# First projections in blocks of 128 rows with a packed rest, lead-in loads shared with SyncE, gradient row copies in the first stage

## The chip, the core and the metric

The kernel runs as one program on one core of a Trainium2 chip. The metric is device time in microseconds (us) of that core; of several runs the median counts. TensorE is called PE in the profile (PEld is its weight load), VectorE DVE, ScalarE ACT, GpSimd POOL and SyncE SP. DMAs are issued from three engines, each with a queue of its own: SP (q1), ACT (q10) and POOL (q0).

## The reference

The kernel computes a forward pass and all gradients of a block with two branches that share a normalized input. Cut to what matters:

```python
xn = layernorm(x)                                  # 2048 tokens x 640
# branch A: 64 segments of 32 tokens; 8 memory rows are carried from one to the next
for s in range(64):
    h = concat([mem, xn[32*s:32*s+32]])            # 40 rows
    q, k, v = h @ Wq, h @ Wk, h @ Wv               # 32 heads x 128
    o = softmax(mask(q @ k.T * 128**-0.5)) @ v
    o = o @ Wo
    mem, out_s = o[:8], o[8:]
# branch B: gated MLP, inner width 1728
g = silu((silu(xn @ w1) * (xn @ w3)) @ w2)
out = x + concat(out_s) * g
# returned: out, and by vjp(grad_out) the gradients of x, mem0, Wq, Wk, Wv, Wo, w1, w3, w2
```

## The kernel before

The program is a row of stages. Inside each of the stages below a helper `in_order` fixes the written order for every engine, so an engine never starts an instruction before the one written ahead of it, and a DMA that has to wait holds up what is written behind it on the same issuing engine. Only semaphores tie the engines together.

**Forward of branch B and the first projections of V** (`phase12_ln_Bfwd`, 0 to 284 us). Layernorm, then the MLP in four blocks of 512 tokens. On the way the normalized rows are copied from DRAM to DRAM into `HRO` in one strided DMA (`x_rows`, L252) on SP. Behind the last block `first_rows` (L358 to L372) computes V for the first 672 tokens (`NB0`) in six blocks of 112 rows. For each block and each of four column groups (`cg`) there are two PSUM banks of 512 columns, and each bank takes five matmuls (L367), one for each 128 of the 640 input features. VectorE evicts the one bank and ScalarE the other into a staging tile `b0st`, and a DMA (L372) stores it. The remaining tokens get their projections one segment at a time in the recurrence, where they ride along with the memory rows.

**First projections of K and Q** (`first_part`, 284 to 407 us). The same `first_rows`, twice 24 steps, counted by `n`. The stores go out on POOL from four staging tiles. In the same steps SP stores the transposed V weights to the DRAM tensor `WVT` (`turn_w`; the tiles lie in a ring of six slots), ACT issues the fetches of Wq and Wo (`fetch`, every other step), POOL clears tiles and loads the memory rows (`mem_ld`), and PE turns the first K rows (`kload`, `kturn`).

**Recurrence** (407 to 1703 us) and a stage of output projections follow. In the recurrence the function `packed_half` (L302 to L308) multiplies 32 rows with four column groups at once: four matmuls of 32 columns of the array each write one quarter of a bank's partitions.

**Backward recurrence** (`phase4_Abwd`, 1888 to 3088 us). It begins with a lead-in of 19 units (`pro`) without a chain. A unit is four heads of up to three segments. Its `ld` loads `qv` (two pieces, L1194 for the memory rows and L266 for the token rows), `gor` (L266) and `Pr` (L1198). In the lead-in `gor` is loaded from SP, and the others from POOL (`early`). `turn` transposes V and the gradient rows; ScalarE copies V out of PSUM (L1209, L1210, two buffers), and POOL stores it to `VTD` (L1211). `dsoft` ends with a store to `DSR` (L1242) on POOL, `gmem` with a store to `GXP` (L1258) on SP. A step `i` of the lead-in does `turn(i)`, `dprob(i-1)`, `dsoft(i-1)`, `gmem(i-2)`, then loads unit `i+4`; in the first eight steps SP also loads an eighth of `WvT` from `WVT`, 640 KB each, and half of a block of `gx_block` (L843) is computed. After the lead-in the chain runs from segment 63 to 0. Behind each step below segment 54 POOL issues one DMA of the list `later` (L1349). Its first two entries copy the gradient rows `GS` to `GWO` from DRAM to DRAM: 21 tiles of 96 rows, 2.58 MB, and a rest of 32 rows. In the chain a step's staging tile `gstg` is stored to `GOS` from SP (L1100), and the same buffer is used again by `fup` (L335) late in the step.

**Weight gradients of branch A** (`phase6_Awgrads`, from 3088 us). Units in the order of `order`; `ld` brings five pieces per unit, and `s1` is the first PE work of a unit (L1426, transposes of `dS`). SP issues the loads of units 0 to 2, then `ld_w(0)`: three weight tiles of 4 heads, the first a plain load from `WVT` (L1394), the other two DMA transposes of Wk and Wq (L271), then the loads of units 3 and 4.

Of the kernel before, what the change touches and what calls it, by code (L numbers as in the profile page):

```python
# [16 lines left out]
P = 128  # L17
# [23 lines left out]
class K:  # L41
# [109 lines left out]
    def setup_dram(self):  # L151
        tc = self.tc
        S, D, T, H, F = self.S, self.D, self.T, self.H, self.F
        HD = self.HD
        dp = self.ctx.enter_context(tc.tile_pool(name="scratch", bufs=1, space=bass.MemoryType.DRAM))
        self.dp = dp
        mk = lambda name, shape, dt=BF16: dp.tile(list(shape), dt, name=name, uniquify=False)
        self.XN = mk("XN", (S, D))
        self.SLT = mk("SLT", (F, S))
        self.DUT = mk("DUT", (F, S))  # L160
        self.HB = mk("HB", (F, S))
        self.DZ = mk("DZ", (S, D))
# [24 lines left out]
        self.GL = 2 * P  # L187
        self.GX0 = mk("GX0", (S - self.GB0, HD))
        self.OR = mk("OR", (self.NTL * 120, HD))
        self.PR, self.DSR, self.VTD = [], [], []  # L190
        self.GXP = mk("GXP", (self.NTL, P, 8, 3, 2, 32), F32)
        for tl in range(self.NTL):
            n = self.geo(tl)[3]
            self.PR.append(mk(f"PR{tl}", (n, H, P)))
            self.DSR.append(mk(f"DSR{tl}", (n, H, P)))
            ns, nm = self.geo(tl)[0:2]
            self.VTD.append(mk(f"VTD{tl}", (P, ns, H, 40)))
        self.PM = mk("PM", (T, P, 80))
        self.GSP = mk("GSP", (8, 3, 160, 512))
        self.WVT = mk("WVT", (P, H, D))  # L200

    def x_src(self, tl, w, c0, c1):
        return self.tok_src(96 * tl, self.geo(tl)[2], w, c0, c1)
# [46 lines left out]
    def x_rows(self, A, X, eng):  # L250
# [2 lines left out]
                      X[0:96 * n, :].rearrange("(t r) d -> t r d", r=96))  # L253
        eng.dma_start(A[120 * n:120 * n + 32, :], X[96 * n:self.S, :])


    def g_src(self, tl, c0, c1):
        nx = self.geo(tl)[2]
# [10 lines left out]
def turned_load(k, dst, src):  # L269

    k.nc.sync.dma_start_transpose(dst, src)  # L271
# [83 lines left out]
    return pt  # L355


def first_rows(k, ps, stage, xs, off, W, dst, x0, cg, nb=112, tag="b0pb", w=1024, q=None):  # L358

    nc = k.nc  # L360
    for b in range(2):
        c0 = cg * 1024 + b * 512
        if w == 512 or b == 0:
            st = stage()
        pb = ps.tile([nb, 512], F32, name="b0pb", tag=tag)
        for dc in range(k.DC):
            nc.tensor.matmul(pb[:], xs[:, dc, x0 - off:x0 - off + nb], W[:, dc, c0:c0 + 512],  # L367
                             start=(dc == 0), stop=(dc == k.DC - 1))
        s0 = b * 512 if w == 1024 else 0
        k.copy(st[:, s0:s0 + 512], pb[:], eng='vs'[b])  # L370
        if w == 512 or b == 1:
            (q or nc.sync).dma_start(dst[x0:x0 + nb, cg * 1024 + (b * 512 if w == 512 else 0):cg * 1024 + b * 512 + 512], st[:])  # L372


def phase3_Afwd(k, W4, Wv, Wk_):
# [18 lines left out]
def first_part(k, Wv, Wk_, Wq, Wo, kTs, vt, hxs, rest):  # L394
    nc, tc = k.nc, k.tc
    DC, H, HD = k.DC, k.H, k.HD
    with tc.tile_pool(name="b0", bufs=1) as io, tc.tile_pool(name="b0s", bufs=4) as stp, \
# [14 lines left out]
        def mem_ld():  # L412
            nc.gpsimd.dma_start(k.m_rows(k.HRO, 0), k.mem0)
            with nc.allow_non_contiguous_dma(reason="tiny mem0 transpose load"):
                for dc in range(DC):
                    nc.gpsimd.dma_start(hxs[0][:, dc, 0:8], k.mem0[:, dc * P:(dc + 1) * P].rearrange("m p -> p m"))
# [31 lines left out]
            turn_w()  # L448
        n = 0
        for W, dst in ((Wk_, k.KX[:, :]), (Wq, k.QVX[:, 0])):  # L450
            for x0 in range(0, k.NB0, 112):
                for cg in range(4):
                    if n % 2 == 1 and fetch:
                        nc.scalar.dma_start(*fetch.pop(0))
                    first_rows(k, ps, lambda: stp.tile([112, 1024], BF16, name="b0st", tag="b0st"), xs, 0, W, dst, x0, cg, q=nc.gpsimd)
                    turn_w()
                    if zero:
                        nc.gpsimd.memset(zero.pop(0)[:], 0.0)
                    if n >= 26 and n % 2 == 0 and (n - 26) // 2 < 9:
                        i = (n - 26) // 2  # L460
                        if i > 0:
                            kturn(i - 1)
                        if i < 8:
                            kload(i)
                    if n == 20:
                        mem_ld()
                    if n == 30:
                        assert not turns
                        nc.gpsimd.memset(kTs[1][:], 0.0)
                    if n == 44:  # L470
                        for i in range(2):
                            nc.sync.dma_start(vt[64 * i + 8:64 * i + 40, :], k.QVX[0:32, 1, 2048 * i:2048 * i + 2048])
                    n += 1
# [375 lines left out]
def phase3b_out(k, Wo, W0, W4):  # L849
# [12 lines left out]
    with tc.tile_pool(name="oio", bufs=1) as io, tc.tile_pool(name="oac", bufs=1, space=bass.MemoryType.PSUM) as pa, \  # L862
# [96 lines left out]
        while g0:  # L959
# [2 lines left out]
        in_order(k, start)  # L962
    WT["v"] = W4.tile([P, H, D], BF16, name="WvT", tag="w3")

    n = k.NTL - 1
    later = [(k.GWO[0:120 * n, :].rearrange("(t r) d -> t r d", r=120)[:, 0:96], k.GS[0:96 * n, :].rearrange("(t r) d -> t r d", r=96)),
             (k.GWO[120 * n:120 * n + 32, :], k.GS[96 * n:k.S, :])]

    for s in range(3):
        t0 = (2, 0, 1)[s]  # L970
# [14 lines left out]
def phase4_Abwd(k, out2, WoT, WvT, WkT, WqT, later):  # L985
# [3 lines left out]
    with tc.tile_pool(name="gst", bufs=1) as st, tc.tile_pool(name="gchain", bufs=1) as ch, \  # L989
# [185 lines left out]
        def ld(tl, qd, eng=None):  # L1175

            ns, nm, nx, n = k.geo(tl)
            c0, h0 = qd * 512, qd * 4
            i = cnt["l"]
            cnt["l"] += 1  # L1180
            early = i < len(pro)
            g = i % 6 if early else (i - len(pro) + 1) % NG
            if g < NG:
                gor = gors[g][:]
                qv = fl.tile([120, 2, 512], BF16, name="gqv", tag="gqv", bufs=4)[:]
                Pr = fl.tile([120, 4, P], BF16, name="gPr", tag="gPr", bufs=4)[:]
            else:
                x = xb[:, g - NG]
                qv = x[:, 0:1024].rearrange("p (i c) -> p i c", i=2)
                gor = x[:, 1024:1536]  # L1190
                Pr = x[:, 1536:2048].rearrange("p (h c) -> p h c", h=4)
            t0 = 3 * tl
            q = nc.gpsimd if early else nc.sync
            q.dma_start(  # L1194
                qv[nx:n], k.QVM[t0:t0 + ns, :, qd // 2, :, 512 * (qd % 2):512 * (qd % 2) + 512].rearrange("t r i c -> (t r) i c"))
            k.load_x(qv, 0, k.x_src(tl, "qv", c0, c0 + 512), q)
            k.load_x(gor, 0, k.g_src(tl, c0, c0 + 512), nc.sync)
            q.dma_start(Pr[0:n], k.PR[tl][:, h0:h0 + 4, :])  # L1198
            uu["l", tl, qd] = qv, gor, Pr

        def turn(tl, qd):
# [152 lines left out]
def phase6_Awgrads(k, X, out0, out3, out4, out5):  # L1354
# [12 lines left out]
    with tc.tile_pool(name="h6i", bufs=3) as io, tc.tile_pool(name="h6", bufs=1) as hp, \  # L1367
# [20 lines left out]
        def ld_w(qd):  # L1388
            c0 = qd * 512
            ws = []  # L1390
            for i, src in enumerate((k.A_Wv, k.A_Wk, k.A_Wq)):
                w = gp.tile([P, 4, D], BF16, name="w6", tag=f"w6{i}")
                if i == 0:
                    nc.sync.dma_start(w[:], k.WVT[:, 4 * qd:4 * qd + 4, :])  # L1394
                else:
                    turned_load(k, w[:], src.rearrange("d h e -> d (h e)")[:, c0:c0 + 512])
                ws.append(w)
            Ws[qd] = ws
# [261 lines left out]
def phase12_ln_Bfwd(k: K, Wv, Wk_):  # L1660
# [6 lines left out]
    with tc.tile_pool(name="bw", bufs=1) as wp, tc.tile_pool(name="bio", bufs=2) as io, \  # L1667
# [162 lines left out]
                            up_ld(blk - 1, fc // 2 + 1)  # L1830
        hidden_out(NBLK - 1)
        xb = io.tile([P, DC, BLK], BF16, name="xnT_b", tag="xnT_b")
        turned_load(k, xb[:, :, 0:224], k.XN[448:672, :])
        up_ld(NBLK - 1, 0)
        up_ld(NBLK - 1, 1)
        xa, off = xnTs[NBLK], 0
        stg = []

        def stage():
            stg.append(ln.tile([112, 512], BF16, name="b0st", tag=f"xt{len(stg) % 8}"))  # L1840
            return stg[-1]
        for n, (x0, cg) in enumerate([(x0, cg) for x0 in range(0, k.NB0, 112) for cg in range(4)]):
            if n % 3 == 1 and n // 3 < TB:
                up(NBLK - 1, n // 3)
                if n < 6:
                    up_ld(NBLK - 1, n // 3 + 2)
            if x0 == 448:
                xa, off = xb, 448
            first_rows(k, ps, stage, xa, off, Wv, k.QVX[:, 1], x0, cg, tag="pg", w=512)
        in_order(k, start)  # L1850


# [271 lines left out]
```

## Time and profile before

| | |
|---|---|
| median of 4 runs | 4889.42 us (4886.75 to 4896.51) |
| the profiled execution | 4891.41 us, its span 4889.7 us |
| busy over the span | PE 93%, PEld 59%, DVE 45%, POOL 41%, ACT 34% |
| DMA | 841 MB, 172 GB/s |

Busy time by stage, from the profile's windows:

| stretch, us | what | PE busy, us | PE clock | DMA share | GB/s |
|---|---|---|---|---|---|
| 205 to 290 | end of branch B, V projections | 75.4 of 85 | 0.99 | 0.49 | 144 |
| 290 to 407 | K and Q projections | 115.3 of 117 | 0.98 | 0.71 | 241 |
| 1893 to 1972 | lead-in of the backward recurrence | 59.2 of 79 | 0.63 | 0.81 | 228 |
| 1975 to 3075 | backward recurrence | 1039.0 of 1100 | 0.98 | 0.71 | 200 |
| 3075 to 4300 | weight gradients of A and what follows | 1190.4 of 1225 | 0.98 | 0.52 | 137 |

A time is that of one whole execution; the span goes from the first to the last instruction of the profiled one. Busy means that at least one instruction of the engine was under way. The clock is the share of full speed that TensorE was granted. The DMA share is the mean busy share of the core's 16 DMA engines; it is modelled and can pass 1.

### The profile page before, as it was taken

What the parts mean: (1) busy time and instruction counts of PE and PEld (TensorE: products, weight loads), DVE (VectorE), ACT (ScalarE), POOL (GpSimd) and SP (SyncE); (2) the same over time, 40 slices, a digit from 0 to 9 for tenths busy, and PEclk for the clock granted to TensorE, in tenths of its full rate; (3) what the DMA queues carried; (4) which work ended last, traced back from release to release, by engine and by line L of the source; (5) the groups of instructions that cost most, each with busy time, mean ns of one, the idle gap of its engine ahead of it and who ended that gap; (6) DMA issues with size and microseconds to landing.
All of it is one profiled execution on the core that took longest, in us unless ns stands there. A gap on an engine that the chain in (4) does not pass through costs nothing. (4 is left out here: it accounts for less than half of the span.)

```text
span 4889.7 us, 160881 instructions
## 1 busy us (share of the span) xinstructions
PE 4543.8 (93%) x64704; PEld 2889.5 (59%) x64704; DVE 2221.5 (45%) x7189; ACT 1686.9 (34%) x4784; POOL 2003.7 (41%) x3384
## 2 busy tenths in 40 slices
PE   8899999999999867889999999799999999999999
PEld 4455555555555554556666665566666666667675
DVE  8634555555555523445555554332333323311461
ACT  5432555555555432323333332222333222300000
POOL 6522444444444313445544444533455334411440
PEclk9999999999999977999999999899999999999999
DMA  8663555555555478677777775743554434659784
GB/s 268 228 231 110 162 169 165 169 163 165 168 160 163 136 166 211 198 202 215 218 211 208 208 204 165 167 121 109 149 152 134 119 107 135 185 173 225 163 182 96
DMA packets 1010341, 841.32 MB, mean 172 GB/s; under 512 B 555979, under 2 KB 893375, under 8 KB 1007591
## 3 DMA queue, kind: packets, MB, share of 16 engines
q1 hardware_dynamic: 783175, 552.52, 41.4%
q0 software_dynamic: 129328, 227.22, 15.9%
q10 hardware_dynamic: 97091, 51.28, 4.2%
q8 instruction: 511, 8.37, 0.8%
q14 instruction: 236, 1.93, 0.1%
HBM read 473.80 MB, written 311.48 MB: 161 GB/s over the span
## 5 line engine op out<-in xcount | busy, mean ns | idle before, releaser
L1505 PE MATMUL wg<-gr,hr 128*128 128x512 bf16 x2400 | 521.7, 379 | 0.0
L1486 PE MATMUL g<-w,ghacc 128*128 128x320 bf16 x3072 | 460.4, 300 | 0.8
L1505 PEld LDWEIGHTS <-hr 128*128 128x128 bf16 x2400 | 233.9, 98 | 278.8
L1486 PEld LDWEIGHTS <-ghacc 128*128 128x128 bf16 x3072 | 288.8, 98 | 104.5 <-ACT ghacc L92 2.2
L738 POOL DMA_DIRECT2D OR<-xv x163 | 93.1, 571 | 446.8 <-ACT xv L737 340.8
L307 PEld LDWEIGHTS <-hx 128*32 128x32 bf16 x7680 | 178.2, 96 | 164.5 <-issue 4.6
L90 DVE CAST wgo<-wg 128x512 bf16<-128x512 f32 x72 | 49.8, 692 | 471.2 <-PE wg L1505 463.2
L90 DVE CAST stg<-bank 128x512 bf16<-128x512 f32 x256 | 177.1, 692 | 183.3 <-PE bank L307 177.7
L92 ACT COPY ghacc<-t6g 128x768 bf16<-128x768 bf16 (+1 forms) x176 | 137.1, 779 | 310.3 <-PE t6g L1468 309.3
L689 ACT ACTIVATE xP<-xsp,xnm 120x120 bf16<-120x120 f32 (+1 forms) x704 | 239.9, 374 | 9.0 <-DVE xnm L685 5.7
L326 PEld LDWEIGHTS <-gkv 128*8 128x8 bf16 x8192 | 178.1, 87 | 84.5 <-issue 4.4
L1211 POOL DMA_DIRECT2D VTD<-gvT x176 | 129.3, 742 | 226.9 <-ACT gvT L1210 205.1
L1451 POOL DMA_DIRECT2D GSP<-grs x48 | 25.7, 548 | 478.3 <-ACT grs L1443 477.5
L700 POOL TENSOR_TENSOR xP<-xP,xrz 120x480 bf16<-120x480 bf16 x163 | 161.8, 993 | 123.3 <-ACT xP L689 82.9
L92 ACT CAST wgo<-wg 128x512 bf16<-128x512 f32 x48 | 28.1, 585 | 479.8 <-PE wg L1505 392.5
L1492 DVE TENSOR_TENSOR ghacc<-ghacc,g 128x320 f32<-128x320 f32 x192 | 93.5, 487 | 209.7 <-PE g L1486 209.7
L1240 DVE SCALAR_TENSOR_TENSOR gdS<-gdp,Dx,gPr 120x120 bf16<-120x120 f32 (+1 forms) x680 | 183.0, 331 | 0.0
L564 DVE COPY vt<-stg 8x512 bf16<-8x512 bf16 x512 | 163.6, 320 | 21.0 <-ACT stg L92 13.5
L1258 POOL DMA_DIRECT2D GXP<-gks x157 | 91.6, 583 | 195.6 <-ACT gks L1256 186.9
L326 PE MATMUL bank<-Wo,oTm 128*32 128x320 bf16 x4032 | 170.4, 321 | 0.4
L326 PE MATMUL gbank<-WvT,gkv 128*8 128x320 bf16 x4096 | 169.5, 309 | 0.6 <-DVE gkv L1082 0.6
L326 PE MATMUL gbank<-WkT,gkv 128*8 128x320 bf16 x4096 | 162.0, 299 | 5.2 <-issue 3.4
(348 smaller groups left out, 10968.5 us busy)
## 6 DMA issues: line engine op xcount, KB each, us to landing
QVS<-stg SPq DMA_DIRECT2D x128, 256.0 KB
vTt<-VTD SPq DMA_DIRECT2D x64, 320.0 KB
VTD<-gvT POOLq DMA_DIRECT2D x168, 120.0 KB, 4.1
DSR<-gdS POOLq DMA_DIRECT2D x168, 120.0 KB, 3.4
dS<-DSR SPq DMA_DIRECT2D x168, 120.0 KB
P<-PR SPq DMA_DIRECT2D x168, 120.0 KB
PR<-xP POOLq DMA_DIRECT2D x163, 120.0 KB, 3.3
OR<-xv POOLq DMA_DIRECT2D x163, 120.0 KB, 2.5
```

Source lines behind the costliest of these rows:

```text
L90: return nc.vector.tensor_copy(out, in_)
L92: return nc.scalar.copy(out, in_)
L307: k.nc.tensor.matmul(bank[32 * g:32 * g + 32, :], x[:, dc, :], W[:, dc, c0:c0 + 512], start=(dc == 0), stop=(dc == k.DC - 1), tile_positio ...
L326: k.nc.tensor.matmul(pm[p0:p0 + nq, 0:320], x[:, h, :], W[:, h, 320 * b:320 * b + 320], start=(first and i == 0), stop=(last and i == 15), ...
L564: nc.vector.tensor_copy(vt[p0:p0 + 8, c0:c0 + 512], sv[32 * g:32 * g + 8, b * 512:(b + 1) * 512])
L689: nc.scalar.activation(Pb[0:n, j, 0:n], sp[0:n, j, :], ACT.Exp, bias=nmx[0:n, j:j + 1], scale=k.scale, accum_out=Z[0:n, j:j + 1])
L700: eng.tensor_tensor(Pb[0:n, :, 0:n], Pb[0:n, :, 0:n], bc_last(rz[0:n], n), ALU.mult)
L1211: nc.gpsimd.dma_start(k.VTD[tl][:, :, h0:h0 + 4, :], vTq[:])
L1240: nc.vector.scalar_tensor_tensor(dS[0:n, j, 0:n], dp[0:n, j, :], Dx[0:n, j:j + 1], Pr[0:n, j, 0:n], op0=ALU.subtract, op1=ALU.mult)
L1486: nc.tensor.matmul(pg[:], ring[:, i, j, r0:r0 + P], Ws[qd][i][:, j, 320 * h:320 * h + 320], start=(i == 0 and j == 0), stop=(i == 2 and j ...
L1492: nc.vector.tensor_tensor(a, a, pg[:], ALU.add)
L1505: nc.tensor.matmul(pw[:], hr[:, tl, dc * P:(dc + 1) * P], grs[i][:, tl, :], start=(tl == 0), stop=(tl == NF - 1))
```

## The change

- `first_rows` takes blocks of 128 rows: five blocks (640 rows). The last 32 rows go through a new function `last_rows`, which uses `packed_half`. The counters at which loads are issued in `first_part` move with the shorter loop (42 steps in place of 48).
- The copies of `GS` to `GWO` leave the list `later`. They are issued from SP in `first_part` at steps 10, 12, 14 and 16, as copies of 6, 6, 6 and 3 tiles and the rest (`x_part`).
- In their places in `later` stand two stores of 640 KB each from the resident transposed Wk and Wq to a new DRAM tensor `WQK`; `ld_w(0)` loads them in place of the two DMA transposes.
- In the lead-in's loads, the token rows of `qv` and `Pr` are issued from SP; the memory rows of `qv` stay on POOL.

```diff
+        self.WQK = mk("WQK", (2, P, 4, D))
...
+    def x_part(self, A, X, i, eng):
+        n = self.NTL - 1
+        h = (n + 3) // 4
+        t0, t1 = h * i, min(h * i + h, n)
+        eng.dma_start(A[120 * t0:120 * t1, :].rearrange("(t r) d -> t r d", r=120)[:, 0:96],
+                      X[96 * t0:96 * t1, :].rearrange("(t r) d -> t r d", r=96))
+        if i == 3:
+            eng.dma_start(A[120 * n:120 * n + 32, :], X[96 * n:self.S, :])
...
-def first_rows(k, ps, stage, xs, off, W, dst, x0, cg, nb=112, tag="b0pb", w=1024, q=None):
+def first_rows(k, ps, stage, xs, off, W, dst, x0, cg, tag="b0pb", w=1024, q=None):
...
-        pb = ps.tile([nb, 512], F32, name="b0pb", tag=tag)
+        pb = ps.tile([P, 512], F32, name="b0pb", tag=tag)
         for dc in range(k.DC):
-            nc.tensor.matmul(pb[:], xs[:, dc, x0 - off:x0 - off + nb], W[:, dc, c0:c0 + 512],
+            nc.tensor.matmul(pb[:], xs[:, dc, x0 - off:x0 - off + P], W[:, dc, c0:c0 + 512],
...
+def last_rows(k, ps, stage, xs, off, W, dst, tag="b0pb", w=1024, q=None):
+    x0 = k.NB0 - 32
+    for b in range(2):
+        if w == 512 or b == 0:
+            st = stage()
+        pb = ps.tile([P, 512], F32, name="b0pb", tag=tag)
+        packed_half(k, pb, xs[:, :, x0 - off:x0 - off + 32], W, b)
+        s0 = b * 512 if w == 1024 else 0
+        k.copy(st[:, s0:s0 + 512], pb[:], eng='vs'[b])
+        if w == 512 or b == 1:
+            c0, c1 = (b * 512 if w == 512 else 0), b * 512 + 512
+            (q or k.nc.sync).dma_start(dst[x0:k.NB0].rearrange("r (g c) -> g r c", g=4)[:, :, c0:c1], st[:])
...
-            for x0 in range(0, k.NB0, 112):
-                for cg in range(4):
+            for x0 in list(range(0, k.NB0 - 32, P)) + [None]:
+                for cg in range(4 if x0 is not None else 1):
...
-                    if n >= 26 and n % 2 == 0 and (n - 26) // 2 < 9:
-                        i = (n - 26) // 2
+                    if n >= 22 and n % 2 == 0 and (n - 22) // 2 < 9:
+                        i = (n - 22) // 2
...
-                    if n == 20:
+                    if n == 18:
                         mem_ld()
+                    if 10 <= n < 18 and n % 2 == 0:
+                        k.x_part(k.GWO, k.GS, (n - 10) // 2, nc.sync)
...
-                    if n == 44:
+                    if n == 38:
...
-    n = k.NTL - 1
-    later = [(k.GWO[0:120 * n, :].rearrange("(t r) d -> t r d", r=120)[:, 0:96], k.GS[0:96 * n, :].rearrange("(t r) d -> t r d", r=96)),
-             (k.GWO[120 * n:120 * n + 32, :], k.GS[96 * n:k.S, :])]
+    later = [(k.WQK[i], WT[w][:, 0:4, :]) for i, w in enumerate("kq")]
...
             q = nc.gpsimd if early else nc.sync
...
-            k.load_x(qv, 0, k.x_src(tl, "qv", c0, c0 + 512), q)
+            k.load_x(qv, 0, k.x_src(tl, "qv", c0, c0 + 512), nc.sync)
             k.load_x(gor, 0, k.g_src(tl, c0, c0 + 512), nc.sync)
-            q.dma_start(Pr[0:n], k.PR[tl][:, h0:h0 + 4, :])
+            nc.sync.dma_start(Pr[0:n], k.PR[tl][:, h0:h0 + 4, :])
...
-                if i == 0:
-                    nc.sync.dma_start(w[:], k.WVT[:, 4 * qd:4 * qd + 4, :])
+                if i == 0 or qd == 0:
+                    nc.sync.dma_start(w[:], k.WVT[:, 4 * qd:4 * qd + 4, :] if i == 0 else k.WQK[i - 1])
                 else:
                     turned_load(k, w[:], src.rearrange("d h e -> d (h e)")[:, c0:c0 + 512])
...
-        for n, (x0, cg) in enumerate([(x0, cg) for x0 in range(0, k.NB0, 112) for cg in range(4)]):
+        for n, (x0, cg) in enumerate([(x0, cg) for x0 in range(0, k.NB0 - 32, P) for cg in range(4)]):
...
+        last_rows(k, ps, stage, xb, BLK, Wv, k.QVX[:, 1], tag="pg", w=512)
```

More of the change, by code (lines that the diff above doesn't have):

```diff
@@ L371, in first_rows @@
         if w == 512 or b == 1:
-            (q or nc.sync).dma_start(dst[x0:x0 + nb, cg * 1024 + (b * 512 if w == 512 else 0):cg * 1024 + b * 512 + 512], st[:])
+            (q or nc.sync).dma_start(dst[x0:x0 + P, cg * 1024 + (b * 512 if w == 512 else 0):cg * 1024 + b * 512 + 512], st[:])
+def last_rows(k, ps, stage, xs, off, W, dst, tag="b0pb", w=1024, q=None):
[10 more added lines that the diff above has]
+            (q or k.nc.sync).dma_start(dst[x0:k.NB0].rearrange("r (g c) -> g r c", g=4)[:, :, c0:c1], st[:])
 def phase3_Afwd(k, W4, Wv, Wk_):
@@ L450, in first_part @@
         for W, dst in ((Wk_, k.KX[:, :]), (Wq, k.QVX[:, 0])):
-            for x0 in range(0, k.NB0, 112):
-                for cg in range(4):
+            for x0 in list(range(0, k.NB0 - 32, P)) + [None]:
+                for cg in range(4 if x0 is not None else 1):
                     if n % 2 == 1 and fetch:
                         nc.scalar.dma_start(*fetch.pop(0))
-                    first_rows(k, ps, lambda: stp.tile([112, 1024], BF16, name="b0st", tag="b0st"), xs, 0, W, dst, x0, cg, q=nc.gpsimd)
+                    stage = lambda: stp.tile([P, 1024], BF16, name="b0st", tag="b0st")
+                    if x0 is None:
+                        last_rows(k, ps, stage, xs, 0, W, dst, q=nc.gpsimd)
+                    else:
+                        first_rows(k, ps, stage, xs, 0, W, dst, x0, cg, q=nc.gpsimd)
                     turn_w()
@@ L1832, in phase12_ln_Bfwd @@
         xb = io.tile([P, DC, BLK], BF16, name="xnT_b", tag="xnT_b")
-        turned_load(k, xb[:, :, 0:224], k.XN[448:672, :])
+        turned_load(k, xb[:, :, 0:160], k.XN[512:672, :])
         up_ld(NBLK - 1, 0)
@@ L1839, in stage @@
         def stage():
-            stg.append(ln.tile([112, 512], BF16, name="b0st", tag=f"xt{len(stg) % 8}"))
+            stg.append(ln.tile([P, 512], BF16, name="b0st", tag=f"xt{len(stg) % 8}"))
             return stg[-1]
-        for n, (x0, cg) in enumerate([(x0, cg) for x0 in range(0, k.NB0, 112) for cg in range(4)]):
+        for n, (x0, cg) in enumerate([(x0, cg) for x0 in range(0, k.NB0 - 32, P) for cg in range(4)]):
             if n % 3 == 1 and n // 3 < TB:
@@ L1846, in phase12_ln_Bfwd @@
                     up_ld(NBLK - 1, n // 3 + 2)
-            if x0 == 448:
-                xa, off = xb, 448
+            if x0 == BLK:
+                xa, off = xb, BLK
             first_rows(k, ps, stage, xa, off, Wv, k.QVX[:, 1], x0, cg, tag="pg", w=512)
+        last_rows(k, ps, stage, xb, BLK, Wv, k.QVX[:, 1], tag="pg", w=512)
         in_order(k, start)
```

## The prediction

> **What bounds the kernel now.** I read the windows first, then, stage by stage, the waits (engine and line, what ended them, us, times, longest) and the timeline. PE is busy 93% of the span, so a stage is worth looking at where its matmuls can be fewer or where PE stands idle. The first projections are of the first kind. The groups of the Q projection, a piece of its timeline (start, duration, engine, line, matmuls merged), and the first packed projections of the recurrence:
>
> ```profile
> L367 PE MATMUL b0pb<-Wq,b0x 128*112 128x512 bf16 x240 | 53.7, 379 | 0.0
> ```
>
> ```profile
> 358.17 6.64 PE L367 MATMUL b0pb<-Wq,b0x 128*112 128x512 bf16 x30
> ...
> 407.20 2.34 PE L307 MATMUL bank<-Wk,hx 128*32 128x512 bf16 x40
> ```
>
> PE never idles there (0.0), and 240 matmuls of 112 rows take 53.7 us, while 40 packed ones take 2.34 us. The same stretch, and those around the backward chain's slow place, the lead-in and the head of the weight gradients, in the windows (PE, PEld, DVE, ACT, POOL busy, clock, DMA share, GB/s):
>
> ```profile
> 316.00:340.00 24.00, 24.00 (x150) 15.24 (x149) 9.18 (x15) 8.82 (x15) 7.57 (x14) 1.00 1.03 384
> ```
>
> ```profile
> 1893.00:1972.00 79.00, 59.16 (x528) 32.78 (x529) 35.33 (x225) 25.19 (x101) 52.18 (x89) 0.63 0.81 228
> 2160.00:2200.00 40.00, 29.62 (x640) 18.20 (x637) 15.22 (x80) 8.42 (x30) 15.51 (x29) 0.92 0.69 204
> 2200.00:2240.00 40.00, 39.04 (x920) 26.28 (x918) 22.10 (x113) 15.17 (x50) 20.24 (x36) 1.00 0.81 231
> ```
>
> PE loses 9.4 us between 2160 and 2200 against the next 40 us. The waits of that place name the copy of `GS` to `GWO` (issued at 2171.5), and those of 1895 to 1985 the lead-in's brake:
>
> ```profile
> ACT fup L335 <- DMA GOS<-gstg: 8.9, 1, 8.9
> POOL GXP L1258 <- DMA GWO<-GS: 8.0, 1, 8.0
> ```
>
> ```profile
> ACT gvT L1209 <- DMA VTD<-gvT: 42.9, 12, 8.2
> ```
>
> A store of 256 KB on another queue landed only with the copy, about 20 us late, and its buffer is the one that `fup` needs. In the lead-in ACT waits for POOL's stores. Last, the head of the weight gradients in the timeline:
>
> ```profile
> 3094.96 5.87 SPq L271 DMA_TRANSPOSE w<-in_A_Wk_dram  x1
> ...
> 3100.87 6.18 SPq L271 DMA_TRANSPOSE w<-in_A_Wq_dram  x1
> ...
> 3107.10 0.59 SPq L1405 DMA_DIRECT2D dS<-DSR  x1
> ...
> 3110.26 0.58 PE L1426 MATMUL t<-ident,dS 120*128 120x120 bf16 x4 [12.75 <-DMA dS<-DSR]
> ```
>
> Two DMA transposes hold SP for 12.05 us, the load of unit 3 stands behind them, and PE idles 12.75 us.
>
> **The change, part by part.** *Blocks of 128 rows.* Each projection loses 40 of its 240 matmuls: (6.64 - 0.38) / 29 = 0.216 us each, 8.64 us. The rest adds 40 packed ones, 2.0 to 2.34 us by the row at 407.20; I take 2.2. Net 6.4 us, for V, K and Q together 19.3 us. Evictions are not slower for 16 rows more: 692 ns for 112x512 and for 128x512 alike, below the 1.08 us of a bank's matmuls. V has two banks and PE waits of 4.2 us for evictions, so 17 is the low end, 20 the high one. [...] The row at 407.20 starts within 0.1 us of the last matmul of 112 rows. [...]
>
> *Copies in the first stage.* Four copies of 6, 6, 6 and 3 tiles go on SP at steps 10 to 16, from about 316 us, two steps of 2.44 us apart. Behind them on SP stand the `WVT` stores, whose ring of six slots covers 14.6 us, and later the `kr` loads, which are used two steps after their issue. On the DMA engines they meet a stretch that is full already (share 1.03): the fetch of Wo, the `KX` stores and `WVT`. PE needs the `KX` stores through the four staging tiles; their slowest landing before is 9.3 us, and then PE lost 1.7 us (14.3 of 16 us busy from 300 to 316). The whole copy took 20.5 us to land at 2171; by bytes a part takes 5.9 us, hence nearly back to back for 24 us. The nearest row is the like copy into `HRO`, the same bytes from the same queue at 164 us: behind it PE lost 5.5 us. Bounds: nothing (PE is busy 24.00 of 24 with the DMA full), and 22 us, four times 5.5; a gain is out, since the copies only add traffic there. I take 6. [...]
>
> *The chain without the copy* gets its 9.4 us back. In the copy's place go two stores of 640 KB on POOL. By bytes each could cost a quarter of 9.4, 4.7 together; or nothing, as the smaller entries of the same list behind 2200, where PE is busy 39.04 of 40. I take 1, nearer to the latter, since the stores read SBUF. Net 8.4.
>
> *Lead-in.* 38 issues of about 0.6 us leave POOL, 23 of its 52 us; on SP they add 38 x 0.4 = 15 us, hidden by SP's own wait for ACT before `GXP` (43.0 us in 13 waits). The `VTD` and `DSR` stores then go out earlier and have less ahead of them on their queue. But every load of unit i+4 now also stands behind `GXP` of unit i-2 and a 640 KB piece of `WvT`; four steps of 3.9 us cover that, against landings of 3.7 to 7.7 us. PE idles 19.8 of 79 us. 6.2 of them go with POOL's wait for `gride`, which stays; of the 13.6 left I take about half, 6. High end 15, what the DMA share of 0.81 leaves free; low end a loss of 5, one late unit.
>
> *Head.* The two loads cost SP 0.9 us instead of 12.05. `dS` of unit 3 is issued at 3095.8, but behind 1.97 MB of weights on its queue. At 384 to 250 GB/s (windows 316 to 340 and 3111 to 3122) these need 5.1 to 7.9 us from 3094.5, and `dS` lands at about 3103 instead of 3110.3: 7.3 us. Low end 3 (202 GB/s as from 3090 to 3098, and 3.2 us to land), high end 11 (3.2 us after its issue).
>
> Sum: 19.3 - 6 + 8.4 + 6 + 7.3 = 35.0 us. From the profiled execution's 4891.4 us that is 4856.4; it lay 2.0 above the median, so 4855 for the median. All favourable ends give 55 us (4834), all unfavourable ones a loss of 2 (4892).
>
> **The rivals.** (1) *The copies starve the first stage*: the term is 22, not 6, the gain 19 us, 4870. For it: the DMA is full there, and both earlier copies of this kind stopped PE. Against it: PE runs two steps ahead in PSUM and four tiles in SBUF. Chance 0.14. (2) *The lead-in is bound by its transfers*: the DMA share is 0.98 from 1910 to 1930, and a wait for the loads takes the place of that for the stores. Term 0, with the head at its low end: 25 us, 4864. Chance 0.12. (3) *Slower*: a part takes as long as the whole copy, because one busy engine and not the bytes set its time. Place: SP and all DMA engines from 316 us. Price: 4 x 20.5 = 82 us, less 4.9 us of steps done in each, 62 us; against the other terms' 41 us that is 21 us slower, 4910. It decides from 13 us of standstill per part (51 us in all). Against it: the nearest copy cost PE 5.5 us in full. Chance 0.03. (4) *It does not matter*: the projections turn out to be held by the full DMA queue, and the stalls return elsewhere, within 0.2%, about 4885. Chance 0.05; PE's idle time of 0.0 speaks against it.
>
> **How the numbers follow.** My forecast, gains of 26 to 46 us, has 0.62, and more than 46 us 0.04. 0.2%, 9.8 us, is about what a measurement of this kernel can tell from no change. Faster by more than that: 0.62 + 0.04 + 0.14 + 0.12 = 0.92; same 0.05; slower 0.03. The range 4839 to 4876 leaves out the last two, part of the first rival's tail, and the best corner.
>
> **What would show it.** In the profile after: 200 matmuls at L367's successor per projection and 40 packed, the three projections 19 us shorter in sum; PE busy near 24 of 24 us where the copies run, or else waits of evictions for `KX` above 14.0 us; no wait of `fup` for `GOS` and about 39 of 40 us busy at the same chain steps; ACT's wait for `VTD` well under 42.9 us; the first wait for `dS` in the head near 5 us. I am wrong if PE loses over 12 us while the copies run, or if the lead-in is no shorter.

## The result and the profile after

The changed kernel takes 4883.52 us (median of 43 runs, 4867.15 to 4895.61) against 4891.76 us (67 runs) of the kernel before on the same chips: a ratio of 0.9983, 95% interval 0.9976 to 0.9990, or 5 to 12 us less. That is within 0.2%, and far from the forecast of 4855. The profiled execution took 4889.7 us, its span 4888.0 us.

The matmuls of the projections are those that were forecast. The groups of the Q projection after:

```profile
L377 PE MATMUL b0pb<-Wq,b0x 128*128 128x512 bf16 x200 | 51.5, 416 | 0.0
...
L317 PE MATMUL b0pb<-Wq,b0x 128*32 128x512 bf16 x40 | 2.3, 380 | 0.0
```

200 and 40 in place of 240. But the mean of one rose from 379 to 416 ns, and the projection as a whole takes 75.4 us (344.81 to 420.23) instead of 54.0: the matmuls lie apart. The windows of the changed kernel (PE, PEld, DVE, ACT, POOL busy, clock, DMA share, GB/s) show where:

```profile
345.00:350.00 5.00, 2.14 (x10) 0.88 (x9) 0.00 (x0) 0.27 (x1) 1.19 (x2) 0.96 0.76 202
350.00:355.00 5.00, 3.41 (x12) 1.52 (x12) 1.69 (x3) 0.34 (x1) 1.31 (x2) 0.50 0.61 188
355.00:360.00 5.00, 4.00 (x19) 1.75 (x18) 0.00 (x0) 1.43 (x3) 0.59 (x1) 0.85 0.34 131
360.00:365.00 5.00, 0.00 (x0) 0.00 (x0) 0.00 (x0) 0.00 (x0) 0.00 (x0) 0.83 0.43 161
```

From 360 to 365 us no engine computes, and the DMA engines, on the mean of all 16, are less than half busy. This is no full DMA. In the kernel before, PE is busy throughout the last two of these windows:

```profile
355.00:360.00 5.00, 5.00 (x32) 3.19 (x31) 2.00 (x4) 1.76 (x3) 1.06 (x2) 1.00 0.72 236
360.00:365.00 5.00, 5.00 (x28) 3.04 (x27) 1.58 (x3) 1.28 (x3) 1.07 (x2) 1.00 0.53 163
```

The waits of 285 to 421 us in the changed kernel say who waits for whom:

```profile
DVE kT L90 <- DMA WVT<-kT: 33.4, 5, 14.3
ACT kT L92 <- DMA WVT<-kT: 27.5, 4, 11.2
PE wpt L451 <- DVE kT L90: 13.0, 2, 8.6
...
PE kpt L468 <- DMA kr<-KX: 6.5, 1, 6.5
```

VectorE and ScalarE stand in front of the ring of six slots, for stores to `WVT` that have not landed. The evictions of the projection stand behind them in the written order, so PE stops. SP's own waits, and a piece of its timeline (start, duration, line), tell why the stores are late:

```profile
SPq L454 <- DMA Wo<-in_A_Wo_dram: 22.5, 2, 19.7
```

```profile
338.41 0.88 SPq L454 DMA_DIRECT2D WVT<-kT  x2
342.83 0.74 SPq L262 DMA_DIRECT2D GWO<-GS  x1
363.32 3.57 SPq L454 DMA_DIRECT2D WVT<-kT  x2
```

After the third copy SP issues no store for 20 us: it waits for a fetch of `Wo` to land. The two have no data in common, but the trace records the completion counters of the DMAs: the 4,662 of SP and ACT share eight, 582 or 583 on each. The store at 363.32 us has the counter of the `Wo` fetch issued at 329.05; the fetch's last update of it comes at 363.22, and SP's wait for that counter ends at 363.25. The second and third copies, issued at 337.56 and 342.83, have those of two earlier `Wo` fetches (issued at 319.30 and 324.63), whose last updates come at 337.54 and 342.81.

The other stages did move as the change meant. The windows of the chain's old slow place, three waits of the lead-in, and the issue of `dS` of unit 3 and its first use in the head:

```profile
2160.00:2200.00 40.00, 36.41 (x854) 23.88 (x855) 18.95 (x94) 12.82 (x44) 18.77 (x34) 1.00 0.80 229
2200.00:2240.00 40.00, 38.59 (x950) 25.54 (x942) 24.37 (x131) 13.52 (x47) 20.34 (x38) 1.00 0.77 219
```

```profile
POOL gox L1059 <- DMA gride<-GS: 12.0, 1, 12.0
PE gvpt L1236 <- DMA gor<-GX: 11.2, 1, 11.2
...
ACT gvT L1238 <- DMA VTD<-gvT: 9.9, 6, 5.0
```

```profile
3095.98 0.49 SPq L1434 DMA_DIRECT2D dS<-DSR  x1
```

```profile
3107.89 0.58 PE L1455 MATMUL t<-ident,dS 120*128 120x120 bf16 x4 [9.57 <-DMA dS<-DSR]
```

PE is busy 36.41 of 40 us instead of 29.62 (the sign named was about 39), and `fup` no longer waits for `GOS`. ACT waits 9.9 us for `VTD` instead of 42.9, but a wait that was small before has grown, that for the `GXP` stores, which stand on SP's queue together with the loads now. Its row before, then after:

```profile
ACT gks L1256 <- DMA GXP<-gks: 4.1, 1, 4.1
```

```profile
ACT gks L1285 <- DMA GXP<-gks: 18.5, 7, 3.4
```

The two DMA transposes are gone, and PE's wait for `dS` fell from 12.75 to 9.57 us.

### The profile page after: what moved, and what is told of

It is laid out like the page before. It is cut to its first block, busy times and chain, and to the rows that moved or that the text cites. A ratio compares the mean times of both kernels' runs of the same rounds, so it can differ in the third digit from the quotient of the medians.

```text
span 4888.0 us, 160803 instructions
## 1 busy us (share of the span) xinstructions
PE 4526.8 (93%) x64704; PEld 2859.1 (58%) x64704; DVE 2214.1 (45%) x7180; ACT 1683.2 (34%) x4775; POOL 1980.9 (41%) x3340
## 3 DMA queue, kind: packets, MB, share of 16 engines
q0 software_dynamic: 127632, 221.55, 15.5%
## 5 line engine op out<-in xcount | busy, mean ns | idle before, releaser
L1269 DVE SCALAR_TENSOR_TENSOR gdS<-gdp,Dx,gPr 120x120 bf16<-120x120 f32 (+1 forms) x680 | 182.9, 331 | 0.0
```

The lines of the kernel that those rows point to most:

```text
L1269: nc.vector.scalar_tensor_tensor(dS[0:n, j, 0:n], dp[0:n, j, :], Dx[0:n, j:j + 1], Pr[0:n, j, 0:n], op0=ALU.subtract, op1=ALU.mult)
```

## Experiments

All times are medians beside runs of the kernel before on the same chip; the ratio is to these. The stage that failed is read as one length, from V's first matmul to the recurrence's first (209.46 to 407.20 before: 197.7 us; 211.19 to 420.06 after: 208.9 us). "The recurrence begins at 422.2" in two expectations below is its row for Wq; its first matmul is at 420.06.

| kernel | time, us (runs) | ratio, 95% interval | first projections, us |
|---|---|---|---|
| before | 4891.76 (67) | | 197.7 |
| after | 4883.52 (43) | 0.9983 (0.9976 to 0.9990) | 208.9 |
| 1 copies back in the chain | 4872.66 (10) | 0.9961 (0.9949 to 0.9974) | 188.6 |
| 2 copies in 16 groups | 4868.72 (6) | 0.9952 (0.9933 to 0.9970) | 194.7 |
| 3 copies in the recurrence | 4863.28 (6) | 0.9941 (0.9922 to 0.9959) | 188.9 |
| 4 WVT stores on POOL | 4872.93 (12) | 0.9965 (0.9953 to 0.9977) | 200.8 |
| 5 as 3, kr later | 4849.52 (4) | 0.9915 (0.9891 to 0.9939) | 182.4 |
| 6 as 5, HRO in 16 groups | 4852.64 (4) | 0.9915 (0.9891 to 0.9939) | 182.0 |
| 7 before, copies alone | 4892.48 (10) | 0.9995 (0.9980 to 1.0011) | 218.9 |
| 8 after, kr later | 4873.15 (9) | 0.9962 (0.9946 to 0.9978) | 203.9 |
| 9 as 8, Wo behind the copies | 4852.84 (4) | 0.9927 (0.9913 to 0.9940) | 188.0 |
| 10 as 8, copies in 16 groups | 4868.20 (4) | 0.9958 (0.9944 to 0.9973) | 192.9 |
| 11 as 5, once more | 4858.40 (5) | 0.9931 (0.9917 to 0.9946) | 182.8 |
| 12 as 6, once more | 4843.10 (4) | 0.9908 (0.9893 to 0.9924) | 182.9 |
| 13 as 8, six groups, short pieces | 4878.23 (10) | 0.9973 (0.9961 to 0.9986) | 207.0 |
| 14 as 8, 96 groups, short pieces | 4866.99 (7) | 0.9954 (0.9939 to 0.9969) | 194.2 |

One of the five runs of 11 took 9003.69 us; the median is of all five (of the other four it is 4855.77), the ratio leaves that run out.

**1: the copies back in the chain.**

```diff
-                    if 10 <= n < 18 and n % 2 == 0:
-                        k.x_part(k.GWO, k.GS, (n - 10) // 2, nc.sync)
...
-    later = [(k.WQK[i], WT[w][:, 0:4, :]) for i, w in enumerate("kq")]
+    n = k.NTL - 1
+    later = [(k.GWO[0:120 * n, :].rearrange("(t r) d -> t r d", r=120)[:, 0:96], k.GS[0:96 * n, :].rearrange("(t r) d -> t r d", r=96)),
+             (k.GWO[120 * n:120 * n + 32, :], k.GS[96 * n:k.S, :])]
+    later += [(k.WQK[i], WT[w][:, 0:4, :]) for i, w in enumerate("kq")]
```

> The four copies leave the first stage; the rows go in two copies in the backward chain as before the change, ahead of the two WQK stores. Theory (the copies held the first stage for about 28 us: the recurrence began at 422.2 instead of the 394 that the shorter projections would give): the recurrence begins near 394, the two projections K and Q end 13 us earlier than before the change, the chain loses its 8 us again, and the time is about 20 us under that of the changed kernel, 4863. Rival A (the blocks of 128 rows cause the stop, because they ask for the KX stores faster): the recurrence still begins near 420 and the time is 8 us above the changed kernel, 4892. Rival B (run to run difference): under 5 us apart.

The recurrence begins at 397.98 us, and the first projections take 188.6 us instead of 208.9: 20 us belong to the copies, not to the blocks of 128 rows. The chain, from its first store to `GWO` to the first transpose of the head, takes 1100.9 us instead of 1087.6. Q still takes 56.3 us (341.89 to 398.15), 2 us more than before the change, with 40 matmuls fewer.

**2: the same copies in 16 groups.**

```diff
-        eng.dma_start(A[120 * t0:120 * t1, :].rearrange("(t r) d -> t r d", r=120)[:, 0:96],
-                      X[96 * t0:96 * t1, :].rearrange("(t r) d -> t r d", r=96))
+        eng.dma_start(A[120 * t0:120 * t1, :].rearrange("(t r) d -> t r d", r=120)[:, 0:96].rearrange("t (p r) d -> p t (r d)", p=16),
+                      X[96 * t0:96 * t1, :].rearrange("(t p r) d -> p t (r d)", p=16, r=6))
```

> The same four copies, of the same bytes, at the same steps and on the same queue, but with 16 groups of 6 rows as their slowest dimension instead of the 6 (or 3) tiles. Theory (few engines): the copy's time is set by the few DMA engines that a slowest dimension of 6 or 3 occupies; spread over all of them each part takes about the 5.9 us that its bytes need, the WVT stores behind it land in time, the recurrence begins between 394 and 400, and the time is 4855 to 4862. Rival (bytes: the stretch is full of traffic and any 2.46 MB more delay it, or SP's queue order alone): the recurrence begins at 415 or later and the time stays within 5 us of the changed kernel.

The recurrence begins at 403.93, neither before 400 nor after 415. DVE's wait for the `WVT` stores is still there, but shorter, as the waits of this kernel show:

```profile
DVE kT L90 <- DMA WVT<-kT: 24.3, 7, 8.9
```

**3: the copies in the recurrence**, one tile for three steps, in 16 groups.

```diff
                 ride_ld(t + 1)
+                if t % 3 == 1 or t == T - 1:
+                    k.x_tile(k.GWO, k.GS, t // 3, nc.sync)
```

> The copies leave the first stage and go into the recurrence, one tile of 96 rows for three steps, each in 16 groups of 6 rows, on SP's queue behind the load of the ride. Theory: the first stage has its 28 us back, the chain keeps its 7 us, and the recurrence, whose windows show a mean of 13 us of PE idle time per 190 us, hides 122,880 bytes per 60 us: 4855. Rival: each copy delays the loads behind it on SP's queue by its own landing, 2 us or more in 22 places, and the time is 4875 or above, with the recurrence longer than the 1290 us from 422.2 to 1712.2 by 20 us or more.

The recurrence from its first matmul to its last Wv half takes 1297.2 us. Kernels without copies in it take 1287.4 to 1296.1, so the copies cost there less than a single profile tells apart. The time stays 8 us above the 4855 expected, and the timeline of the Q projection shows why:

```profile
350.84 2.32 PE L385 MATMUL b0pb<-Wq,b0x 128*128 128x512 bf16 x10
352.99 0.44 PE L459 MATMUL wpt<-ident,Wv 128*128 128x128 bf16 x5
358.96 0.50 PE L476 MATMUL kpt<-ident,kr 96*128 96x96 bf16 x4 [5.52 <-DMA kr<-KX]
359.26 4.47 PE L385 MATMUL b0pb<-Wq,b0x 128*128 128x512 bf16 x10
```

The first turn of `kr` stands in PE's order at step 24 and its load at step 22; before the change they stood at 28 and 26, behind the last `WVT` store and the fetches. PE stands for 5.52 us, and the next ten matmuls run at half the clock (4.47 us instead of 2.32).

**4: the WVT stores on POOL's queue**, with the copies where the change put them.

```diff
-            nc.sync.dma_start(k.WVT[:, h, :], sl)
+            nc.gpsimd.dma_start(k.WVT[:, h, :], sl)
```

> The copies stay as the change has them; the 32 stores of the turned weights (WVT) go from SP's queue to POOL's. Theory Q (order on SP's queue: the WVT stores stand behind the copies, their six slots run dry, and VectorE and ScalarE stand in the evictions of the weight turns with the evictions of the projection behind them): the WVT stores now pass the copies, the stop goes, the recurrence begins before 402 and the time is 4858 to 4865. Theory E (the engines: any transfer of 128 rows needs also the engines that the copies hold, whatever its queue): the WVT stores still take 11 us and more to land, the recurrence begins after 412 and the time is within 8 us of the changed kernel.

408.8 us lies between the two theories. The waits for `WVT` fell (DVE's longest from 14.3 to 7.4 us), and those for the projection's own stores, which were on POOL's queue all the time, took their place:

```profile
DVE b0st L90 <- DMA KX<-b0st: 31.7, 11, 12.1
ACT b0st L92 <- DMA KX<-b0st: 25.2, 6, 11.6
```

So the stop does not go when the `WVT` stores leave SP's queue. This run alone cannot say why, since POOL's queue now carries the 32 `WVT` stores between the projection's own; the single pieces below bear on what both queues wait for.

**5, 8 and 7: each loss by itself.** In 5 and 8 the loads and turns of `kr` go three steps later, in 5 on the kernel of experiment 3 and in 8 on the changed kernel:

```diff
-                    if n >= 22 and n % 2 == 0 and (n - 22) // 2 < 9:
-                        i = (n - 22) // 2
+                    if n >= 25 and n % 2 == 1:
+                        i = (n - 25) // 2
```

> The kernel with the copies in the recurrence, and the eight loads and turns of kr three steps later (from step 25 instead of 22). Theory: what is left of the first stage's loss is the first turn of kr. It stands in PE's order at step 24, its load left SP only at 356.3 us behind a wait for Wo, PE stood 5.5 us, and the clock was at half for 2 us of work after it; so the Q projection takes 48 to 49 us instead of 56.3, the recurrence begins 7 us earlier, and the time is 4855 to 4857. Rival: the wait for Wo only moves to the next load of SP, the Q projection still takes over 53 us, and the time is within 3 us of 4863.

> The changed kernel with its copies where the change put them, and the kr loads and turns three steps later. Theory A (two separate losses): the wait of PE for kr (6.5 us) goes, the recurrence begins at 412 and the time is 4875. Theory B (the copies' stop covers it: SP is behind for both, and a later kr stands behind the same queue): the recurrence begins within 3 us of 420 and the time stays near 4883.

In 5 the Q projection takes 48.8 us (341.92 to 390.71), PE never waits for `kr`, and the first projections take 182.4 us instead of 188.9. In 8 they take 203.9 instead of 208.9. So `kr` costs 5 to 6.5 us with the copies and without, and it is a loss of its own (theory A). The copies cost 203.9 - 182.4 = 21.5 us between these two.

Experiment 7 puts the four copies, and nothing else of the change, into the kernel before:

> The kernel before, with one change alone: the copies leave the chain and go into the first stage in four parts, at the same steps 10 to 16. Theory (the price belongs to the copies and their place): the recurrence begins 20 us later, at 427, the chain gets 9 us back, and the time is 10 us above the kernel before, 4901. Rival (only together with the blocks of 128 rows, which ask for the KX stores and the WVT slots sooner): the recurrence begins before 415 and the time is under that of the kernel before.

The first projections take 218.9 us, 21.2 more than before. The same wait shows in this kernel:

```profile
DVE kT L90 <- DMA WVT<-kT: 34.6, 5, 14.3
```

The price is that of the copies in this place, with blocks of 112 rows as well as of 128. The chain got 10.6 us back (1083.8 instead of 1094.4), and the time is the same as before (ratio 0.9995), not the 4901 expected.

**9: Wo behind the copies.** The four fetches of `Wo` move from steps 11 to 17 to steps 27 to 39; the copies stay as in the change, six tiles long.

```diff
-                    if n % 2 == 1 and fetch:
+                    if fetch and (n % 2 == 1 if len(fetch) > 4 else n >= 27 and n % 4 == 3):
```

> The kernel with the kr loads three steps later and the copies where the change put them; the four loads of Wo (1280 KB each) go from steps 11 to 17, between the copies, to steps 27 to 39, behind them. What is open: whether a copy on few DMA engines is slow by itself, or because it shares those engines with Wo and the stores. Theory M (meeting: Wo's pieces on the copies' engines land late, SP's stores wait for them, up to 18.3 us): with Wo out of the way SP's waits for Wo go, the copies cost under 8 us instead of 21, the recurrence begins at 399 or before (412.65 with Wo between them, 391.4 without the copies), and the time is 4862 or less. Theory S (the copies alone hold the queue for about 20 us each, or 24 us by their bytes): the stop stays, the recurrence begins at 407 or later, 4868 or more. Either way the late Wo may delay the kr loads by some us.

188.0 us instead of 203.9. SP issues copies and stores without a stop, and the windows of 355 to 365 us are filled again. Timeline of SP and windows of 9, then the same windows of 8:

```profile
319.10 0.80 SPq L262 DMA_DIRECT2D GWO<-GS  x1
320.00 2.06 SPq L454 DMA_DIRECT2D WVT<-kT  x2
322.11 0.75 SPq L262 DMA_DIRECT2D GWO<-GS  x1
```

```profile
355.00:360.00 5.00, 5.00 (x21) 2.30 (x20) 2.48 (x4) 1.67 (x3) 1.12 (x3) 0.66 0.61 230
360.00:365.00 5.00, 4.25 (x24) 1.87 (x23) 1.33 (x4) 1.17 (x2) 1.08 (x2) 1.00 0.85 221
```

```profile
355.00:360.00 5.00, 0.62 (x3) 0.20 (x2) 0.00 (x0) 0.00 (x0) 0.00 (x0) 0.92 0.39 151
360.00:365.00 5.00, 1.04 (x7) 0.77 (x7) 1.59 (x3) 0.18 (x1) 0.00 (x0) 0.50 0.40 142
```

16 of the 21.5 us come from the meeting with `Wo`, not from the copies alone (theory M). A late `Wo` without the copies was not run, but it could win little by itself: in 5, without copies, PE stands only 2.9 us in the K and Q projections (102.0 of 104.9 us busy).

**10, 13 and 14: groups or pieces.** 10 is experiment 2 with the late `kr`. 13 has six groups with rows of 1,280 bytes as contiguous pieces, 14 has 96 groups with the same pieces. The edits in `x_part`, 13 and then 14:

```diff
+        for o in range(2):
+            eng.dma_start(A[120 * t0:120 * t1, :].rearrange("(t r) d -> t r d", r=120)[:, o:96:2],
+                          X[96 * t0:96 * t1, :].rearrange("(t r) d -> t r d", r=96)[:, o:96:2])
...
+        eng.dma_start(A[120 * t0:120 * t1, :].rearrange("(t r) d -> t r d", r=120)[:, 0:96].rearrange("t (p r) d -> p r t d", p=16),
+                      X[96 * t0:96 * t1, :].rearrange("(t p r) d -> p r t d", p=16, r=6))
```

> The smallest mending of the change: its copies at their steps, in 16 groups of 6 rows, and the kr loads three steps later. If the two losses are separate, the recurrence begins at 403.9 - 8 = 396 and the time is 4857 to 4861; if the copies, split or not, hide the wait for kr, the recurrence begins after 401 and the time is 4866 or more.

> The kernel with the late kr loads and the copies where the change put them, but each part as two copies, of the even and of the odd rows: the slowest dimension stays 6 (or 3) tiles, and the contiguous pieces are rows of 1,280 bytes instead of halves of tiles of 61,440. From V's first matmul to the recurrence's first that kernel takes 203.9 us with the long pieces, 192.9 us with 16 groups (whose pieces are 7,680 bytes), 182.4 us without copies. Theory N (the number of engines): with six groups it stays at 200 us or more, time 4870 or more. Theory P (the long pieces, behind which the pieces of Wo and of the stores wait on the same engines): it falls to 195 us or less, time 4865 or less.

> The same kernel, each part as one copy of 96 groups of 6 (or 3) rows of 1,280 bytes: the slowest dimension is a multiple of 16, the pieces are as short as in the run beside it. Theory N: near the 192.9 us of the 16 groups with pieces of 7,680 bytes, 188 to 197, and at least 5 us under the run with six groups. Theory P: within 3 us of the run with six groups, both at 195 or less.

10 goes by the second branch of its expectation: the recurrence begins at 403.08 us, and the late `kr` gains 1.8 us there, not 8, so in experiment 2 the wait for `kr` was mostly covered, and 16 groups cost 192.9 - 182.4 = 10.5 us, half of the 21.5. 13 takes 207.0 us, 14 takes 194.2. The number of groups decides, not the length of the pieces. In 13 the DMA share falls to the same height as in 8:

```profile
355.00:360.00 5.00, 0.00 (x0) 0.00 (x0) 0.00 (x0) 0.00 (x0) 0.00 (x0) 0.65 0.39 129
```

0.39 is near 6/16 = 0.375, the share of six busy engines of sixteen.

The trace's records of single DMA pieces show six at work at a time, and also that a copy is not slow by itself. The first copy after the change moves its twelve pieces of 61,440 bytes six at a time, about 2.3 us each, and is through in 5.7 us (326.8 to 332.5). But in 8, from 355 to 360 us, hardly a piece of a copy is left, and yet just six pieces are under way during 69% of the time and seven during 23%. They belong to the `Wo` fetch and to POOL's stores. After the change, from 360 to 365 us, between the last piece of the third copy (358.3) and the first of the fourth (368.5), six are under way during 49%, five during 23% and seven during 16%. The trace does not number the engines: that both stand in line at the six that the copies had loaded, while the other ten are idle, is read from these counts and the shares of 0.39 and 0.43. The last piece of `Wo` lands at 349.9 us before the change, at 366.1 after it, at 362.5 in 8, at 358.5 in 10, and at 351.4 and 354.7 without copies (5 and 11).

**6, 11 and 12: the HRO copy as well.** The copy of the input rows at 164 us has 21 tiles as its slowest dimension. In 6 and 12 it has 16 groups; 11 and 12 repeat 5 and 6 side by side.

```diff
-        eng.dma_start(A[0:120 * n, :].rearrange("(t r) d -> t r d", r=120)[:, 0:96],
-                      X[0:96 * n, :].rearrange("(t r) d -> t r d", r=96))
+        eng.dma_start(A[0:120 * n, :].rearrange("(t r) d -> t r d", r=120)[:, 0:96].rearrange("t (p r) d -> p t (r d)", p=16),
+                      X[0:96 * n, :].rearrange("(t p r) d -> p t (r d)", p=16, r=6))
```

> The same, and the copy of the input rows into HRO at 164 us also in 16 groups of rows. PE lost 5.5 us behind that copy in the trace of before. Theory (few engines set a copy's time): V's projection begins 3 to 5 us earlier, at 205 to 206 instead of 209.5, and the time is 3 to 5 us under that of the kernel without it. Rival: the copy is hidden there, V begins within 1.5 us of 209.5.

> The kernel with the copies in the recurrence and the late kr loads, once more, beside the next one: 4848 to 4856, the first projection of V from 209 us on.

> The same with the HRO copy in 16 groups, once more. In its trace V began 7.4 us earlier (201.7 instead of 209.0) and the span was 5 us shorter, but the two medians of 4 runs each were 3 us apart the other way. If the split is worth what the trace shows: 5 to 8 us under the kernel beside it, and V from 202 us on. If the 7.4 us are this one profile's: V near 209 and no difference.

V's first matmul is at 201.66 and 201.51 us with the groups, at 209.02 and 208.87 without: 7.4 us in both pairs, more than the 3 to 5 expected. The medians alone would not tell it (3 us more in the first pair, 15 less in the second). Windows of the kernel before, then of 12:

```profile
180.00:184.00 4.00, 3.73 (x22) 1.98 (x21) 0.00 (x0) 0.70 (x1) 0.00 (x0) 1.00 0.41 149
184.00:188.00 4.00, 0.00 (x0) 0.00 (x0) 0.26 (x1) 0.00 (x0) 0.53 (x1) 0.79 0.45 175
```

```profile
180.00:184.00 4.00, 4.00 (x23) 2.06 (x21) 3.83 (x7) 0.70 (x1) 3.45 (x6) 1.00 0.71 271
184.00:188.00 4.00, 4.00 (x29) 2.56 (x27) 3.09 (x7) 3.25 (x7) 3.23 (x5) 1.00 0.28 111
```

The 7.4 us match what PE lost behind that copy before: a stand of 5.55 us, and about 2 us in the ten matmuls after it (4.4 us for what takes 2.4 elsewhere). This version, the change with its copies in the recurrence, `kr` later and both copies in 16 groups, has the lowest ratios, 0.9915 and 0.9908, but by their intervals it is not told apart from 5 (0.9915) and hardly from 11 (0.9931).

## Why the prediction was wrong, point by point

The step that failed is the term of the **copies in the first stage**: sized 6 us, it is 20 to 21.5 us (after against 1, 8 against 5, 7 against before). Its high end and the first rival's price, 22 us, came within 2 us of it. The choice of 6, "nearest" to the 5.5 us behind the `HRO` copy, was not: that copy meets no fetch of 5 MB. The text named the fetch of Wo, the stores and the ring of six slots, but weighed them by bytes and by a DMA share of 1.03. The profile after has a share of 0.34 to 0.43 while everything waits. The third rival's mechanism, that busy engines and not bytes set the time, was the right kind; its 20.5 us for each part was not, since a part is through in 5.7 us, and with `Wo` out of the way all four cost 188.0 - 182.4 = 5.6 us. What the copies delay is the fetch beside them (last piece at 362.5 us in 8, at 351.4 in 5). (The 24 us "nearly back to back" count the fourth part as a full one; by the same row all four are 20.5 us. The sum does not use them.) PE was busy 15.5 us from 345 to 380, so it lost 19.5 us, over the 12 named as the mark of a wrong forecast.

A term was **missing**. The change moves the `kr` loads to step 22, ahead of the last `WVT` stores and into the end of the fetch. The prediction gave the move no price; it is 5 to 6.5 us.

**Projections**: forecast 19.3, measured 15 (197.7 to 182.4 and 182.8, without copies and with `kr` late). V is 6.4 us shorter (74.2 to 67.8) as forecast. But the K projection's first block then waits 5.3 us for `b0x` instead of 2.2, so 3 of these are given back:

```profile
PE b0pb L377 <- DMA b0x<-XN: 5.3, 1, 5.3
```

The packed rest costs what was taken for it: its row is 2.34 us long, and the next matmul starts 2.16 us after it (417.90 to 420.06 in the profile after), against 2.2. Its start in the timeline of experiment 3:

```profile
393.20 4.48 PE L385 MATMUL b0pb<-Wq,b0x 128*128 128x512 bf16 x20
397.62 2.34 PE L325 MATMUL b0pb<-Wq,b0x 128*32 128x512 bf16 x40
```

It begins at 397.62, and the full matmuls before it end at 397.68 (ends are modelled; at 0.216 us each, 20 from 393.20 would let the next start at 397.52). So at most 0.1 us is lost here at the change from full to packed matmuls.

**Chain**: forecast 8.4. From its first store to `GWO` to the head's first transpose it takes 1094.4 us before; with the `WQK` stores and without the copies 1077.6 to 1088.4 in thirteen profiles, mean 1084.3, hence 10.1. Without the `WQK` stores (7) it takes 1083.8, so they cost nothing that shows.

**Lead-in**: forecast 6. From the first store of `GWO` by SP to the chain's first it takes 106.6 and 101.9 us without the change (before and 7), 98.5 to 103.0 with it (mean 100.6 of fourteen): 3.6 us against the mean of the two. The wait for `VTD` went as foreseen; the one for `gride`, taken as staying at 6.2 us, became 12.0, and that of PE for `gor` went from 9.3 to 11.2. ACT's wait for `GXP` rose from 4.1 to 18.5 us, which takes back much of what `VTD` gave. The prediction saw the loads standing behind the `GXP` stores on SP, not the stores behind the loads. So waits for the loads, and for stores behind the loads, took a part of the old place, in part as in the second rival; no run here changed the loads to prove it.

**Head**: forecast 7.3, measured from the first transpose to the first gradient matmul: 23.9 and 21.8 us without, 17.8 to 20.3 with it (mean of fourteen 19.3), against the mean 22.85 of the two 3.5 us less, near the low end of 3. `dS` was issued at 3095.98 as forecast, but landed 11.9 us later instead of 7.2. From 3094 to 3108 us the DMA share is 0.97 at 262 GB/s, 3.7 MB, where the term counted 1.97 MB of weights ahead of `dS`; it left out the other loads.

The sum of the measured terms is -15 + 6 + 20.5 - 10.1 - 3.6 - 3.5 = -6 us; measured are -5 to -12. So no term of size is missing from this list. Single profiles differ by some us in stages that no edit touched (the recurrence 1287 to 1297 us), so terms below 3 us are not told apart here.

What is not shown: how the remaining 10.5 us of the copies in 16 groups divide into bytes and SP's order (`Wo` lands 4 to 7 us later in 10 than in 11 and 5, which speaks for bytes as a part), and how much the eight completion counters add by themselves, since the program was not built without them.

## What to carry to other kernels

Before moving a DRAM-to-DRAM copy beside other traffic, look at its slowest dimension: here copies of six groups had six pieces under way at a time and one of 21 groups seven, and the `Wo` fetch beside those of six landed 11 us later (362.5 instead of 351.4 us, 8 against 5); 16 groups cured half of it here (21.5 to 10.5 us), and a place without a big fetch three quarters (to 5.6). When a loop gets shorter, follow each load whose step number moves with it to what its queue carries at the new time. A stall with a DMA share far under 1 (0.34 to 0.43) was here a sign of few busy engines, and the wait that explained it was the issuing engine's own.

## What the runs showed of the hardware

- Around a copy with few groups the DMA share fell near its count of pieces under way, over 16, and stayed there for other queues' pieces after its own were through: 0.39 with 6 groups (6/16 = 0.375; exactly six pieces under way in 69% of 355 to 360 us in 8), 0.41 to 0.45 with 21 (7/16 = 0.44; the `HRO` copy's 42 pieces of 61,440 bytes go seven at a time, and exactly seven of others are under way in 74% of 184 to 188 us before, when the copy had ended).
- The length of a contiguous piece, 61,440 or 1,280 bytes, made no gain in copies of six groups (203.9 and 207.0 us); pieces of 7,680 and 1,280 bytes in 16 or 96 groups were alike too (192.9 and 194.2).
- After a stand of 5.5 us PE took 4.47 us for ten matmuls that take 2.32, so this wait cost some 2 us on top of itself. The trace grants half the clock from 357.0 to 363.8 us there, 4.8 us of them after PE's restart at 358.96.
